# Block 2 moved to the scaled form, and layer 0's weight bound taken from row sums on ScalarE

## The chip, the cores and the metric

The kernel runs on one core of one Trainium2 chip. The metric is the device time of one execution in microseconds (us), from the core's first to its last instruction with the little that lies around it; it is compared as a median of several executions. A core has five engines that work side by side, each through its own instructions in order: TensorE (PE in the profile, matmuls into PSUM), ScalarE (ACT, one function over a tile), VectorE (DVE, elementwise work and reductions), GpSimd (POOL), and SyncE (SP), which here issues most DMAs. An instruction that waits holds back all that stand behind it on its engine.

## The reference, cut to what matters

```
x: (2, 4096, 192)   weight: (8, 7)   w_in: (192, 2048)   w_out: (2048, 192), each layer has its own
w   = softmax(weight)                               # 7 taps per head
x   = causal convolution of x along the 4096 with w, as (8192, 192)
h   = x @ moe_w_in;  g = h * sigmoid(h);  x = g @ moe_w_out                    # layer 0 (SiLU)
h   = x @ moe2_w_in; g = where(h > 0, h, exp(min(h, 0)) - 1); return g @ moe2_w_out   # layer 1 (ELU)
```

All of it is fp32. The kernel keeps fp32 accuracy by splitting each operand of a product in a high part (fp32r, what TensorE reads in one pass) and a low part (the rest), and by adding three products: high by high, high by low and low by high.

## The kernel before

**Tiling.** The 8192 tokens are cut in 16 blocks b of 512, and the 2048 hidden columns in 8 chunks q of 256. A unit (layer, b, q) makes a PSUM tile `h` of 128 x 1024 from the block's tokens and the chunk's `w_in` (18 matmuls of 64 rows by 512 columns, two on the array at a time, L554), then ScalarE and VectorE make `g` in a high and a low part, then TensorE multiplies these by the chunk's `w_out` into sums in PSUM that run over the 8 chunks. `h` has two buffers (`ps_h`, L81): the `in` products of unit s+2 cannot start before unit s's `h` has been read for the last time.

**Two forms of a unit.** The *plain* form (`act_steps`, L579 to L584) makes `hi` and `g` by two SiLU passes on ScalarE and `lo = g - hi` on VectorE, and its `out_products` (L621, L714) are 20 fp32 matmuls. The *scaled* form (L585 to L596) makes one SiLU, then `hi = s * g` (ScalarE, L588), then a 16-bit `lo` (VectorE, L591), with a power of two `s` (`forth`) that keeps `lo` in range. Its `high_products` (L648) are 12 fp32 matmuls; the low products of all 8 chunks are made together at the block's end from 16-bit tiles (`low_products`, L686: 64 matmuls at L671 and L681). `scaled()` (L414) says that all of layer 1 and, in layer 0, the blocks from `NEW` = 3 take this form.

**What the scaled form needs.** For `forth` of a block: a bound on its tokens (`measure`, L432: two VectorE reductions, then a DMA `share` to DRAM and, some steps later, a DMA `fetch` that brings all rows' values to every partition, both on SP's queue) and a bound on the layer's weights. For layer 0's weights `measure_w` (L234) makes 16 reductions on VectorE, `set_weight_scale` (L468) combines them (the tile `own`), and `share` and `fetch` go over GpSimd's queue; `finish_weight_scale` (L479) makes the scales `up` and `down` on VectorE. `set_scale` (L456) makes `forth` and `back`. Each chunk's `w_out` must then be rescaled: `rescale(q)` (L248) has two ScalarE copies (the first makes the 16-bit `w16`), one VectorE instruction (`more`) and two GpSimd additions; `rescale_end(q)` (L261) is one more ScalarE copy. A block's sums are taken out of PSUM by `end_steps` and `emit_end_c`.

**Order.** The order is written out by hand. `units` (L825) lists the units of all blocks, and step s of the program emits the `in` products of unit s. Blocks 0 and 1 go in turn, one chunk each (steps 0 to 15); block 2 has steps 16 to 23 (`TWO` = 16), block 3 steps 24 to 31, and so on. In steps 3 to 18 `both_products` (L1085) interleaves unit s's `in` products with the `out` products of unit s-3. `pair_products` (L714) lets the two row halves of the array add into the same bank, so the second half must come after the first: SP carries a small instruction (`mark`, L743) that waits for a matmul of the first half, and a matmul of the second half waits for that mark. There are three marks a step, in SP's order among its DMAs. From step 20 the loop (L1134) emits `in` products of s, then the work hung into the step by `at(step, f)` (`run_fill`), then the activation of s, then the `out` or `high` products of unit s-2, and of s-3 after the step `turn` = 26 (`LAG` = 2, `LATE` = 3, L822).

Within steps 4 to 18 each step goes: matmuls; in even steps to 12 `decode_steps` of chunk s/2+1, 64-bit data to fp32: ScalarE writes the scratch tile `mag` (L144), VectorE makes two parts (L147, L151) and joins them with `mag` (L155), which is the last to read it; in odd steps `split_w` (two ScalarE copies, three GpSimd subtractions); then what is hung into the step; then the activation. All chunks of layer 0 use one and the same `mag` (`mag_0`, L980). In these steps ScalarE's two SiLUs of unit s free its `h`, since `g` goes to SBUF (`in_tmp`); from step 19 on `g` stays in `h`, and VectorE's `lo` frees it. The plan hangs the 14 taps of block 2's convolution into steps 6 to 13 and those of block 3 into 14 to 20 (`spread`, L871), with the split of the block in high and low (`split_conv`) at the end; block 2's crossing DMAs are put into `pending` and go out behind marks.

Of the kernel before, what the change touches and what calls it, by code (L numbers as in the profile page):

```python
# [9 lines left out]
F32 = mybir.dt.float32  # L10
# [35 lines left out]
def kernel(  # L46
# [184 lines left out]
        t = w16_t[layer, q] = w16_p.tile([P, 2, D], F16, tag=f"w16_{layer}_{q}", name="w16")  # L231
        return t

    def measure_w(q):  # L234
        wi, wo = wt[0, q]
        for k, w in enumerate((wi[:, 0, :], wo[:, :, 0:D])):
            nc.vector.tensor_reduce(
                out=found[:, k, q : q + 1], in_=w.bitcast(F32), axis=AX.X if k == 0 else AX.XY, op=ALU.max,
                apply_absolute_value=True,
            )  # L240
# [592 lines left out]
    def at(step, f, part=0):  # L833
        fill.setdefault((max(step, 0), part), []).append(f)
# [28 lines left out]
    for b in range(2, NB):  # L863
        s = where[0, b, 0]
        if b > 2:
            at(s - 14, lambda b=b: pending.extend(x_loads(b)) if b < 5 else load_x(b))
        steps = [f for fs in zip(*(conv_steps(b, g) for g in range(2))) for f in fs]
        found_it = [lambda b=b: measure(0, b, conv_t[b, 0], conv_t[b, 1])]
        splits = [lambda b=b, g=g: split_conv(b, g) for g in range(2)]
        if b <= 3:  # L870
            spread(steps + found_it * (b == NEW) + splits, s - 10, 7 if b > 2 else 8)  # L871
        elif b == 4:
            for k, f in enumerate(steps):
                at((22, 22, 22, 23, 23, 23, 24, 24, 24, 24, 25, 26, 27, 27)[k], f)
            at(s - 5, found_it[0])
        else:
            for k, f in enumerate(steps):
                step = s - 8 if k < 1 else s - 7 if k < 2 else s - 6
                at(step, f, 0 if k < 5 else 1 if k < 10 else 2)
            at(s - 5, found_it[0])  # L880
        if b >= NEW:
            soon = b in (4, 5)
            at(s - 3 - soon, lambda b=b: fetch((0, b)))
            at(s - 1 - soon, lambda b=b: set_scale(0, b))
        if b >= 4:
            for f in splits:
                at(s - 4, f)
# [3 lines left out]
        at(where[1, b, 0] - 4 - (b == 0), lambda b=b: fetch((1, b)))  # L891
        at(where[1, b, 0] - 2, lambda b=b: set_scale(1, b))
    for q in range(NQ):
        at(TWO - 2 + q // 3, lambda q=q: measure_w(q))
    at(TWO, lambda: set_weight_scale(0, found))
    at(TWO + 1, lambda: fetch(0, nc.gpsimd))
    at(TWO + LAG, lambda: finish_weight_scale(0))
# [25 lines left out]
    with tc.manual_schedule():  # L923
# [301 lines left out]
```

## Time and profile before

| | |
|---|---|
| time, median of 3 (lowest, highest) | 1072.87 us (1072.59, 1072.89) |
| profiled execution: time, span | 1072.07 us, 1070.4 us |
| PE busy | 1065.1 us (100%) |
| DVE busy | 820.0 us (77%) |
| ACT busy | 814.1 us (76%) |
| POOL busy | 89.7 us (8%) |
| granted TensorE clock | 1.000 (mean of the span) |

The profile covers one execution. Times are counted from the span's start. Busy time is when an engine had an instruction at work; matmuls overlap, so that of PE is not a measure of how well it is used: here two matmuls run at a time, and what a group of them takes is read from the start of one group to the start of the next. The difference of 1.7 us between the profiled execution's time and its span lies outside the kernel's instructions.

### The profile page before, as it was taken

What the parts mean: (1) busy time and instruction counts of PE and PEld (TensorE: products, weight loads), DVE (VectorE), ACT (ScalarE), POOL (GpSimd) and SP (SyncE); (2) the same over time, 40 slices, a digit from 0 to 9 for tenths busy, and PEclk for the clock granted to TensorE, in tenths of its full rate; (3) what the DMA queues carried; (4) which work ended last, traced back from release to release, by engine and by line L of the source; (5) the groups of instructions that cost most, each with busy time, mean ns of one, the idle gap of its engine ahead of it and who ended that gap; (6) DMA issues with size and microseconds to landing.
All of it is one profiled execution on the core that took longest, in us unless ns stands there. A gap on an engine that the chain in (4) does not pass through costs nothing.

```text
span 1070.4 us, 23207 instructions
## 1 busy us (share of the span) xinstructions
PE 1065.1 (100%) x9763; PEld 830.7 (78%) x9763; DVE 820.0 (77%) x1123; ACT 814.1 (76%) x908; POOL 89.7 (8%) x139
## 2 busy tenths in 40 slices
PE   9999999999999999999999999999999999999998
PEld 6999977777778777777777787777777777877776
DVE  8998867887877878777467777777777777777766
ACT  7766866666667766677688888888988888888885
POOL 5521121100111011100100000000000000000000
PEclk9999999999999999999999999999999999999999
DMA  6423156424333342323641122311122211222100
GB/s 163 134 46 85 31 137 156 124 71 99 99 109 95 95 116 85 111 76 85 188 123 36 26 59 60 60 41 44 37 60 60 59 37 26 60 60 60 40 13 19
DMA packets 48760, 82.64 MB, mean 77 GB/s; under 512 B 10576, under 2 KB 22736, under 8 KB 48656
## 3 DMA queue, kind: packets, MB, share of 16 engines
q1 hardware_dynamic: 42416, 57.30, 22.1%
q0 software_dynamic: 6240, 23.86, 7.4%
q8 instruction: 76, 1.25, 0.6%
q14 instruction: 28, 0.23, 0.1%
HBM read 43.23 MB, written 18.12 MB: 57 GB/s over the span
## 4 chain that ended last, share of the span: by engine, by line
PE 97%; DMA 1%; DVE 1%; SPq 0%; ACT 0%; issue 0%; DVEq 0%
PE h L554 48%; PE ab L659 20%; PE c L659 10%; PE ab L681 9%; PE c L671 5%; PE ab L734 2%; PE c L734 1%; PE ab L640 1%; PE c L640 1%; DMA raw<-in_w_dram 0%; PE last L698 0%; DMA x_hl<-x_hl 0%; SPq L304 0%; DVE lo L591 0%; ACT x L1013 0%
## 5 line engine op out<-in xcount | busy, mean ns | idle before, releaser
L554 PE MATMUL h<-x_hl,wi 64*128 64x512 f32 x4464 | 575.4, 389 | 0.4 <-DMA x_hl<-x_hl 0.2
L554 PEld LDWEIGHTS h<-x_hl,wi 64*128 64x128 f32 x4464 | 438.4, 184 | 85.5 <-DMA x_hl<-x_hl 0.7
L600 DVE SCALAR_TENSOR_TENSOR g<-g,h 128x1024 f32<-128x1024 f32 x128 | 156.3, 1221 | 127.6 <-ACT g L599 127.6
L659 PE MATMUL ab<-g_hi,wo 64*128 64x512 f32 x1856 | 248.1, 386 | 0.0
L659 PEld LDWEIGHTS ab<-g_hi,wo 64*128 64x128 f32 x1856 | 174.0, 184 | 36.5
L591 DVE SCALAR_TENSOR_TENSOR lo<-h,forth,g_hi 128x1024 f16<-128x1024 f32 x104 | 133.4, 1282 | 84.5 <-ACT g_hi L588 84.0
L596 ACT ACTIVATE h<-h 128x1024 f32<-128x1024 f32 x104 | 104.8, 1008 | 86.0 <-PE h L554 85.9
L591 DVE SCALAR_TENSOR_TENSOR lo<-g,forth,g_hi 128x1024 f16<-128x1024 f32 x128 | 163.6, 1278 | 0.0
L598 ACT ACTIVATE g<-h 128x1024 f32<-128x1024 f32 x128 | 131.6, 1028 | 39.2 <-PE h L554 39.2
L659 PE MATMUL c<-g_hi,wo 64*128 64x512 f32 x928 | 143.2, 386 | 0.0
L588 ACT ACTIVATE g_hi<-g,forth 128x1024 fp32r<-128x1024 f32 x126 | 143.1, 1136 | 0.0
L599 ACT ACTIVATE g<-g 128x1024 f32<-128x1024 f32 x128 | 135.7, 1060 | 4.1
L588 ACT ACTIVATE g_hi<-h,forth 128x1024 fp32r<-128x1024 f32 x104 | 116.2, 1117 | 3.4
L681 PE MATMUL ab<-lo,w 64*128 64x512 f16 x900 | 102.2, 377 | 0.0
L659 PEld LDWEIGHTS c<-g_hi,wo 64*128 64x128 f32 x928 | 87.0, 184 | 18.5 <-DVE g_hi L607 0.2
L509 DVE SCALAR_TENSOR_TENSOR conv<-x_raw,tap_w,conv 128x512 f32<-128x512 f32 (+1 forms) x174 | 100.5, 632 | 0.2
L681 PEld LDWEIGHTS <-w 64*128 64x128 f16 x900 | 41.4, 94 | 58.2 <-issue 11.8
L671 PE MATMUL c<-lo,w 64*64 64x512 f16 x928 | 55.7, 379 | 0.0
L671 PEld LDWEIGHTS <-w 64*64 64x64 f16 x928 | 24.5, 106 | 27.4 <-issue 10.2
L581 ACT ACTIVATE g_hi<-h 128x1024 fp32r<-128x1024 f32 x22 | 22.5, 1023 | 23.7 <-PE h L554 23.7
L789 ACT ACTIVATE mid_ab<-ab,back 128x512 f32<-128x512 f32 x13 | 9.0, 690 | 35.1 <-PE ab L681 35.1
L789 ACT ACTIVATE o<-ab,back 128x512 f32<-128x512 f32 x16 | 11.0, 690 | 32.2 <-PE ab L681 28.4
(132 smaller groups left out, 844.2 us busy)
## 6 DMA issues: line engine op xcount, KB each, us to landing
x_hl<-x_hl SPq DMA_DIRECT2D x60, 256.0 KB, 3.8
raw<-in_w_dram POOLq DMA_DIRECT2D x16, 512.0 KB, 4.6
x_raw<-in_xT_dram SPq DMA_DIRECT2D x16, 259.0 KB, 4.3
kept_ab<-mid_ab SPq DMA_DIRECT2D x16, 256.0 KB, 2.1
raw<-in_w_dram POOLq DMA_DIRECT2D x32, 128.0 KB, 3.7
mid_ab<-kept_ab SPq DMA_DIRECT2D x16, 256.0 KB, 5.1
mid_c<-kept_c SPq DMA_DIRECT2D x32, 128.0 KB, 5.0
x_hl<-x_hl SPq DMA_DIRECT2D x30, 128.0 KB, 3.8
```

Of the source, the lines that this page charges most:

```text
L509: nc.vector.scalar_tensor_tensor(out=y, in0=x, scalar=w, in1=y, op0=ALU.mult, op1=ALU.add)
L554: nc.tensor.matmul(out=h[:, r, :], lhsT=w[ROWS[r], w_lo, ts(of, P)], rhs=x_part(layer, b, 3 * x_lo + part)[ROWS[r], :], start=n == 0, stop ...
L588: nc.scalar.activation(out=hi, in_=g, func=ACTF.Copy, scale=s)
L591: nc.vector.scalar_tensor_tensor(out=lo, in0=g, scalar=s, in1=hi.bitcast(F32), op0=ALU.mult, op1=ALU.subtract)
L596: return [lambda: begun.append(nc.scalar.activation(out=g, in_=h, func=ACTF.Silu)), high, low]
L598: lambda: begun.append(nc.scalar.activation(out=g, in_=h, func=ACTF.Relu, scale=-1.0)),
L599: lambda: nc.scalar.activation(out=g, in_=g, func=ACTF.Exp, scale=-1.0),
L600: lambda: nc.vector.scalar_tensor_tensor(out=g, in0=g, scalar=-1.0, in1=h, op0=ALU.add, op1=ALU.max),
L659: nc.tensor.matmul(out=acc_t[layer, b, f"{name}{r}"], lhsT=wo[ROWS[r], i, ts(k, P)], rhs=hi[ROWS[r], i, :], start=q == 0 and n in (0, 2), ...
L671: nc.tensor.matmul(out=acc_t[layer, b, f"c{r}"][ROWS[i], :], lhsT=w16_t[layer, q][ROWS[r], i, P:D], rhs=g_t[u][1][ROWS[r], i, :], start=Fa ...
L681: nc.tensor.matmul(out=acc_t[layer, b, f"ab{r}"], lhsT=w16_t[layer, q][ROWS[r], i, 0:P], rhs=g_t[u][1][ROWS[r], i, :], start=False, stop=l ...
L734: ins = nc.tensor.matmul(out=acc_t[0, b, name][0 : cols.stop - cols.start, :], lhsT=wo[ROWS[r], i, cols], rhs=g_t[0, b, q][part][ROWS[r], ...
```

## The change

`NEW` becomes 2, so block 2 takes the scaled form: 8 units lose 8 of their 20 `out` matmuls, and `low_products` stands at the block's end. Block 2's tokens are measured (step 12), its `share` and `fetch` (step 13) go over SP, and its scales are set in step 15, behind that step's other work. The weight bound is no longer the maximum over the weights (16 reductions on VectorE in steps 14 to 16) but the largest sum of magnitudes of a row: `sum_w(q)` on ScalarE, one ACTIVATE over 128 x 768 that also gives its sum, or for chunks 0 to 2 (whose decoded tile is gone by then) two over 128 x 384. Their elementwise output goes into `mag`, where nobody reads it. They stand in steps 7, 9, 11, 6, 8, 10, 12, 13 for q = 0 to 7. `set_weight_scale`, `fetch` and `finish_weight_scale` move from steps 16, 17, 18 to 13, 14, 15. `rescale(q)` moves from steps 19 to 24, 28 and 30 to steps 16 to 23, and `rescale_end(q)` to the step after each. The weight `fetch` gets a tile of its own. Around step 19 the `out` products of units 16 and 17 give way to the `high` products of unit 16, so that the lag of three steps begins with block 2; `turn` falls on step 18, where it has no effect.

```
--- before.py
+++ after.py
@@ -36,7 +36,8 @@
 PLACES = NQ + 1
 LINE = 128
 C_LO = HP + 2
-NEW = 3
+NEW = 2
+EARLY = 3
 RING = 11
 EXP = 0x7F800000
 TINY = 2.0**-60
@@ -231,13 +232,21 @@
         t = w16_t[layer, q] = w16_p.tile([P, 2, D], F16, tag=f"w16_{layer}_{q}", name="w16")
         return t
 
-    def measure_w(q):
+    sums = []
+
+    def sum_w(q):
+
+        mag, val = dec_t[0, q]
         wi, wo = wt[0, q]
-        for k, w in enumerate((wi[:, 0, :], wo[:, :, 0:D])):
-            nc.vector.tensor_reduce(
-                out=found[:, k, q : q + 1], in_=w.bitcast(F32), axis=AX.X if k == 0 else AX.XY, op=ALU.max,
-                apply_absolute_value=True,
-            )
+        if q < EARLY:
+            of = [(t[:, IN], w.bitcast(F32)) for t, w in ((mag, wi[:, 0, :]), (mag, wo[:, :, 0:D]))]
+        else:
+            of = [(mag, val.bitcast(F32))]
+        for to, w in of:
+            if len(w.shape) == 3:
+                to = to.rearrange("p (i d) -> p i d", d=D)
+            nc.scalar.activation(out=to, in_=w, func=ACTF.Abs, accum_out=found_0[:, len(sums) : len(sums) + 1])
+            sums.append(q)
 
     def measure_raw(q):
         t = raw_t[1, q].bitcast(F32).rearrange("p (g n two) -> p g n two", g=2, two=2)
@@ -262,6 +271,7 @@
         nc.scalar.activation(out=wt[0, q][1][:, :, 0:D], in_=w16_t[0, q], func=ACTF.Copy)
 
     found = fixed.tile([P, 2, NQ], F32, name="found")
+    found_0 = fixed.tile([P, NQ + EARLY], F32, name="found_0")
 
     tap_raw = const.tile([P, 2, TAPS], F32, name="tap_raw")
     tap_e = const.tile([P, 2, TAPS], F32, name="tap_e")
@@ -425,7 +435,7 @@
         queue.dma_start(out=shared[key].rearrange("a (p n) -> (a p) n", n=2), in_=t)
 
     def fetch(key, queue=nc.sync):
-        t = fixed.tile([P, 2 * P], F32, tag="all", name="all")
+        t = fixed.tile([P, 2 * P], F32, tag="all" if type(key) is tuple else "every", name="all")
         queue.dma_start(out=t, in_=shared[key].to_broadcast([P, 2 * P]))
         shared[key] = t
 
@@ -868,7 +878,7 @@
         found_it = [lambda b=b: measure(0, b, conv_t[b, 0], conv_t[b, 1])]
         splits = [lambda b=b, g=g: split_conv(b, g) for g in range(2)]
         if b <= 3:
-            spread(steps + found_it * (b == NEW) + splits, s - 10, 7 if b > 2 else 8)
+            spread(steps + found_it + splits, s - 10, 7 if b > 2 else 8)
         elif b == 4:
             for k, f in enumerate(steps):
                 at((22, 22, 22, 23, 23, 23, 24, 24, 24, 24, 25, 26, 27, 27)[k], f)
@@ -881,7 +891,7 @@
         if b >= NEW:
             soon = b in (4, 5)
             at(s - 3 - soon, lambda b=b: fetch((0, b)))
-            at(s - 1 - soon, lambda b=b: set_scale(0, b))
+            at(s - 1 - soon, lambda b=b: set_scale(0, b), int(b == NEW))
         if b >= 4:
             for f in splits:
                 at(s - 4, f)
@@ -891,14 +901,13 @@
         at(where[1, b, 0] - 4 - (b == 0), lambda b=b: fetch((1, b)))
         at(where[1, b, 0] - 2, lambda b=b: set_scale(1, b))
     for q in range(NQ):
-        at(TWO - 2 + q // 3, lambda q=q: measure_w(q))
-    at(TWO, lambda: set_weight_scale(0, found))
-    at(TWO + 1, lambda: fetch(0, nc.gpsimd))
-    at(TWO + LAG, lambda: finish_weight_scale(0))
+        at((7, 9, 11, 6, 8, 10, 12, 13)[q], lambda q=q: sum_w(q))
+    at(TWO - 3, lambda: set_weight_scale(0, found_0.unsqueeze(1).to_broadcast([P, 2, NQ + EARLY])))
+    at(TWO - 2, lambda: fetch(0, nc.gpsimd))
+    at(TWO - 1, lambda: finish_weight_scale(0))
     for q in range(NQ):
-        step = TWO + LAG + 1 + q + (q > 5) * (q - 3)
-        at(step, lambda q=q: rescale(q))
-        at(step + 1 + 5 * (q == 5), lambda q=q: rescale_end(q))
+        at(TWO + q, lambda q=q: rescale(q))
+        at(TWO + q + 1, lambda q=q: rescale_end(q))
     looks = [(b, *n) for b in range(3, 6) for n in ((7, 13), (8, 14), (9, 16))][:NQ]
     looks[:3] = (3, 9, 13), (3, 10, 14), (3, 11, 16)
     for q, (b, load, look) in enumerate(looks):
@@ -1124,11 +1133,10 @@
         for f in pending:
             f()
         products(in_products(units[TWO + 3]))
-        products(out_products(units[TWO]))
         act = act_steps(units[TWO + 3])
         run_fill(TWO + 3)
         run(act)
-        products(out_products(units[TWO + 1]))
+        products(high_products(units[TWO]))
 
         turn = where[0, NEW, 0] + LAG
         for s in range(TWO + 4, n_units):
```

## Rows read from the trace of the kernel before

**Rows 1.** The page, busy us (share of the span) and instructions of each engine

```profile
PE 1065.1 (100%) x9763; PEld 830.7 (78%) x9763; DVE 820.0 (77%) x1123; ACT 814.1 (76%) x908; POOL 89.7 (8%) x139
```

**Rows 2.** Windows: stretch, length; busy us of PE, PEld, DVE, ACT, POOL; PEclk; DMA

```profile
77.50:99.60 22.10, 22.10 (x199) 21.86 (x197) 21.51 (x41) 13.21 (x18) 2.30 (x4) 1.00 0.20 61
38.00:90.00 52.00, 52.00 (x462) 51.43 (x460) 48.35 (x69) 31.29 (x40) 16.02 (x15) 1.00 0.25 67
```

**Rows 3.** Timeline of TensorE: start, length, what, count; groups that open steps

```profile
90.53 2.36 PE L554 MATMUL h<-x_hl,wi 64*128 64x512 f32 x18
...
101.41 2.36 PE L554 MATMUL h<-x_hl,wi 64*128 64x512 f32 x18
...
135.81 2.20 PE L554 MATMUL h<-x_hl,wi 64*128 64x512 f32 x18
...
139.21 2.20 PE L554 MATMUL h<-x_hl,wi 64*128 64x512 f32 x18
...
158.03 2.43 PE L554 MATMUL h<-x_hl,wi 64*128 64x512 f32 x18
...
190.69 1.50 PE L554 MATMUL h<-x_hl,wi 64*128 64x512 f32 x10
```

**Rows 4.** Timeline of ScalarE, steps 6 to 8; in brackets the idle time before

```profile
36.98 0.91 ACT L144 ACTIVATE mag<-raw 128x768 f32<-128x768 f32 x1
39.05 1.03 ACT L581 ACTIVATE g_hi<-h 128x1024 fp32r<-128x1024 f32 x1 [1.16 <-PE h L554]
39.97 1.02 ACT L582 ACTIVATE g<-h 128x1024 f32<-128x1024 f32 x1
...
41.31 0.51 ACT L179 ACTIVATE wo<-val 128x384 fp32r<-128x384 f32 x1
43.35 1.03 ACT L581 ACTIVATE g_hi<-h 128x1024 fp32r<-128x1024 f32 x1 [1.53 <-PE h L554]
...
47.66 1.03 ACT L581 ACTIVATE g_hi<-h 128x1024 fp32r<-128x1024 f32 x1 [1.57 <-PE h L554]
```

**Rows 5.** Timeline of VectorE, steps 6 to 8, and block 2's split

```profile
39.89 0.96 DVE L155 SCALAR_TENSOR_TENSOR val<-mag,val 128x768 int32<-128x768 int32 x1
...
45.33 1.23 DVE L583 TENSOR_TENSOR g_lo<-g,g_hi 128x1024 fp32r<-128x1024 f32 x1 [0.66 <-ACT g L582]
46.48 0.61 DVE L147 TENSOR_SCALAR val<-raw 128x768 uint16<-128x768 uint16 x1
...
47.67 0.96 DVE L155 SCALAR_TENSOR_TENSOR val<-mag,val 128x768 int32<-128x768 int32 x1
...
68.21 2.80 DVE L166 TENSOR_TENSOR x_hl<-conv,x_hl 128x512 fp32r<-128x512 f32 x3
```

**Rows 6.** Waits of SP's queue from 20 to 100 us: total, times, longest

```profile
SPq L743 <- PE ab L734: 41.0, 30, 2.2
...
SPq L425 <- DVE sum L435: 3.4, 1, 3.4
```

**Rows 7.** Timeline of VectorE, the weight bound's round trip and unit 19

```profile
85.89 0.17 DVE L471 TENSOR_REDUCE own<-found 128x2 f32<-128x16 f32 x1
...
94.29 0.42 DVE L481 TENSOR_REDUCE most<-all 128x2 f32<-128x256 f32 x1 [0.18 <-DMA all<-shared]
...
98.35 1.22 DVE L583 TENSOR_TENSOR g_lo<-h,g_hi 128x1024 fp32r<-128x1024 f32 x1
```

**Rows 8.** Timeline of ScalarE, the split of block 3 in step 20

```profile
98.19 1.36 ACT L163 ACTIVATE x_hl<-conv 128x512 fp32r<-128x512 f32 x3
```

**Rows 9.** Groups by shape, 0 to 150 us: count, busy us, mean ns, idle before

```profile
L254 DVE SCALAR_TENSOR_TENSOR more<-wo,up,w 128x384 f32<-128x384 f32 x8 | 4.9, 612 | 0.1
L252 ACT ACTIVATE w<-wo,up 128x384 f16<-128x384 f32 x8 | 4.9, 606 | 2.7 <-DVE up L445 2.6
...
L237 DVE TENSOR_REDUCE found<-wi 128x1 f32<-128x384 f32 x8 | 4.3, 544 | 0.0
...
L262 ACT ACTIVATE wo<-w 128x384 fp32r<-128x384 f16 x8 | 4.1, 517 | 0.7 <-DVE more L254 0.6
```

**Rows 10.** One line's instructions: ns min/median/max, start; ScalarE's smallest ACTIVATE

```profile
L279 ACT ACTIVATE tap_e<-tap_e x1: 216/216/216, 3.0 to 3.0; 128x14 f32<-128x14 f32 x1
```

More of the change, by code (lines that the diff above doesn't have):

```diff
@@ L38 @@
 C_LO = HP + 2
-NEW = 3
+NEW = 2
+EARLY = 3
 RING = 11
@@ L232, in new_w16, with sum_w @@
         return t
-    def measure_w(q):
+    sums = []
+    def sum_w(q):
+        mag, val = dec_t[0, q]
         wi, wo = wt[0, q]
[L236 to L240, printed above, removed]
+        if q < EARLY:
+            of = [(t[:, IN], w.bitcast(F32)) for t, w in ((mag, wi[:, 0, :]), (mag, wo[:, :, 0:D]))]
+        else:
+            of = [(mag, val.bitcast(F32))]
+        for to, w in of:
+            if len(w.shape) == 3:
+                to = to.rearrange("p (i d) -> p i d", d=D)
+            nc.scalar.activation(out=to, in_=w, func=ACTF.Abs, accum_out=found_0[:, len(sums) : len(sums) + 1])
+            sums.append(q)
     def measure_raw(q):
@@ L264 @@
     found = fixed.tile([P, 2, NQ], F32, name="found")
+    found_0 = fixed.tile([P, NQ + EARLY], F32, name="found_0")
     tap_raw = const.tile([P, 2, TAPS], F32, name="tap_raw")
@@ L427, in fetch @@
     def fetch(key, queue=nc.sync):
-        t = fixed.tile([P, 2 * P], F32, tag="all", name="all")
+        t = fixed.tile([P, 2 * P], F32, tag="all" if type(key) is tuple else "every", name="all")
         queue.dma_start(out=t, in_=shared[key].to_broadcast([P, 2 * P]))
@@ L870 @@
         if b <= 3:
-            spread(steps + found_it * (b == NEW) + splits, s - 10, 7 if b > 2 else 8)
+            spread(steps + found_it + splits, s - 10, 7 if b > 2 else 8)
         elif b == 4:
@@ L893 @@
     for q in range(NQ):
[L894 to L897, printed above, removed]
+        at((7, 9, 11, 6, 8, 10, 12, 13)[q], lambda q=q: sum_w(q))
+    at(TWO - 3, lambda: set_weight_scale(0, found_0.unsqueeze(1).to_broadcast([P, 2, NQ + EARLY])))
+    at(TWO - 2, lambda: fetch(0, nc.gpsimd))
+    at(TWO - 1, lambda: finish_weight_scale(0))
     for q in range(NQ):
-        step = TWO + LAG + 1 + q + (q > 5) * (q - 3)
-        at(step, lambda q=q: rescale(q))
-        at(step + 1 + 5 * (q == 5), lambda q=q: rescale_end(q))
+        at(TWO + q, lambda q=q: rescale(q))
+        at(TWO + q + 1, lambda q=q: rescale_end(q))
     looks = [(b, *n) for b in range(3, 6) for n in ((7, 13), (8, 14), (9, 16))][:NQ]
@@ L1126 @@
         products(in_products(units[TWO + 3]))
-        products(out_products(units[TWO]))
         act = act_steps(units[TWO + 3])
@@ L1130 @@
         run(act)
-        products(out_products(units[TWO + 1]))
+        products(high_products(units[TWO]))
         turn = where[0, NEW, 0] + LAG
```

2 lines of the change are left out of this document (1 added, 1 removed).

## The prediction

> **What bounds the kernel now.** The page's busy times come first [rows 1]: TensorE is busy all the span, VectorE and ScalarE three quarters of it. Second, TensorE's timeline [rows 3]: groups follow each other at even distances, so any matmul taken away shortens the span, and any wait put in front of TensorE lengthens it. Third, windows around the change [rows 2]: from 38 to 90 us VectorE works 48.35 of 52 us and ScalarE 31.29; from 77.5 to 99.6 VectorE works 21.51 of 22.1. The changed steps thus lie where VectorE has nothing to spare, and the question is who then waits for whom in order. Fourth, the timelines of ScalarE and VectorE in steps 6 to 8 [rows 4, 5]: the slack is ScalarE's idle time ahead of each SiLU, 1.16 to 1.57 us a step.
>
> A step up to 18 takes 4.30 us (the SiLUs of units 6, 7, 8 start at 39.05, 43.35, 47.66 [rows 4]); step s+1 opens 0.2 us before unit s's SiLU. Step 19 opens at 90.53 [rows 3]; counted back by 4.307, step 8 opens at 43.15, 10 at 51.76, 12 at 60.37, 13 at 64.68.
>
> **1. Fewer matmuls: -2.4.** From step 19 to block 4's third unit TensorE takes 158.03 - 90.53 = 67.50 us. A scaled block's period is 190.69 - 158.03 = 32.66 [rows 3]. Two of them, without the 0.23 us that the first group after low products is longer (2.43 against 2.20), are 65.1. This also holds the loss around the present switch at step 26.
>
> **2. The sums on ScalarE: +3.2 by step 12.** Chunks 3 to 6 are summed in even steps 6, 8, 10, 12, behind that step's decode, and write `mag`. VectorE's joining instruction (L155) of the next chunk reads `mag`, so the sum waits for it, and the SiLUs, which free `h`, stand behind the sum on ScalarE. Who waits for these: TensorE, two steps on.
>
> A sum over 768 columns has no row. Below: the same ACTIVATE without a sum, 0.91 [rows 4]. Above: one more small instruction for the sum, at most the smallest ACTIVATE's 0.22 [rows 10]. A saving is excluded, as each is an added instruction. I take 0.1, since neighbours on ScalarE overlap by about 0.1 (SiLU starts 39.05 and 39.97, length 1.03), so a sum holds the engine for 0.9 and a pair of SiLUs ends 1.95 after it starts.
>
> Step 6: VectorE's join ends at 39.89 + 0.96 = 40.85 [rows 5]; sum to 41.8, SiLUs to 43.75. Step 8 wanted `h` at 43.15: 0.6 late.
>
> From there a round of two steps goes: ScalarE's two copies 0.83 (the last ends at 41.82, the SiLUs ended at 40.99 [rows 4]), two sums over 384 of 0.5 each (0.52 by the copy of that size [rows 9]), SiLUs 1.95, together 3.8; VectorE's `lo` 1.15, two decode instructions 1.19, join 0.96 [rows 5], 3.3; sum 0.9, SiLUs 1.95. Sum 9.9, where two steps are 8.61: 1.3 late each round, at steps 10 and 12. Unit 8's SiLUs end at 53.7, unit 10's at 63.6. Together 0.6 + 1.3 + 1.3 = 3.2. Without the waits at `mag` the sums would fit in ScalarE's idle time.
>
> **3. Block 2's measure behind SP's marks: +2.5.** In step 12 `share` waits on SP for two reductions on VectorE; such a wait took 3.4 us for block 3, where no marks are left, and marks make up most of SP's waits [rows 6]. Behind it stand step 13's marks, and TensorE's second row half waits for the first of them. Unit 11's SiLUs end 3.8 after 63.6, at 67.3; chunk 7's join at 70.6; one tap and two reductions (0.54 for 384 columns [rows 9]; an estimate of 1.3 for 768 columns and the tap) make 71.9; issuing the DMA 0.4, 72.4. TensorE wants the mark nine pairs, 2.0 us, into step 13: 64.68 + 3.2 + 2.0 = 69.9. So 2.5 late, which covers the 1.3 that ScalarE would cost at step 14. The `fetch` of step 13 waits for the landing on the same queue; I expect it past in time, bounds 0 and 1. Step 14 is then 5.75 us late.
>
> **4. The weight bound's round trip and VectorE's queue: +3.5.** The combined bound `own` follows unit 12's SiLUs (70.6 + 0.9 + 1.95 = 73.5), `lo` 1.15 and block 2's split, 2.8 to 3.1 [rows 5]: at about 77.8. From `own` to the first use of what comes back took 94.29 - 85.89 = 8.4 [rows 7], so VectorE is held at `finish_weight_scale` in step 15 until 86.2. Queued behind it: unit 15's `lo`, the taps, all to unit 19's `lo`. How much is that? Before, the stretch from step 15 to unit 19's `lo` held 21.5 us of VectorE's work [rows 2]. It loses ten reductions and `own` (4.7), gains three `more` (0.53 each after overlap [rows 9]) and block 2's scale (estimate 1.4, six small instructions), and 0.9 of taps stand ahead of the wait: 18.9, with about 1.7 of waiting for ScalarE in units 17 and 19. Unit 19's `lo` ends at 106.8. A scaled step takes 139.21 - 135.81 = 3.40 [rows 3], so TensorE wants unit 19's `h` at 90.53 + 5.75 + 6.8 = 103.1: 3.5 late after rounding. Before, that `lo` ended at 99.6 and was wanted at 101.41 [rows 3, 7]: step 19 held two `out` groups, which was its cover, and is gone.
>
> **5. Rescaling in steps of 3.40 us: +2.9.** ScalarE's step 20 to 23 is an end copy 0.41, two copies 0.51 each, all less the overlap [rows 9], SiLU and `hi` 1.05 each (an estimate from the 1.02 of a SiLU over the same tile [rows 4]): 3.5 against 3.40, so 0.1 late in steps 23 and 24; step 20 also has block 3's split of 1.36 [rows 8], which makes step 22 1.5 late. In steps 23 and 24 VectorE has block 3's scale and seven taps ahead of `lo`: step 25 is 1.2 late. Then block 2's low products (5.1 us of TensorE alone) let both engines catch up.
>
> **Nothing, with what hides it.** GpSimd's additions are done two steps ahead of their `high` products; GpSimd is nearly idle there [rows 2]. `rescale_end` likewise. PSUM is emptied at block 2's end under the low products, as at block 3's. If that cover failed, it would cost under 1 us.
>
> **Sum.** 3.2 + 2.5 + 3.5 + 2.9 - 2.4 = +9.7. From the profiled execution's 1072.07 that is 1081.8; the median lies 0.8 above that execution, so 1082.5.
>
> **Unknown sizes.** The sum's price of 0 to 0.22 more moves this by -1 to +1.2 (seven sums gate a step). The round trip may be 1 shorter or longer, one to one. Block 2's split is slow in its row, 2.8 us for three instructions [rows 5], beside GpSimd's work; if it and the taps of odd steps go at full speed, 1.2 less.
>
> **Rivals.**
> A. VectorE's relief wins, *not slower*. Sixteen reductions at 0.46 (0.54 less overlap [rows 9]) free VectorE 7.4 us in steps 14 to 16, and ScalarE has 20.7 us idle from 38 to 90 [rows 2]; if VectorE's decode did not stand behind the preceding `lo`, unit 8's SiLUs would end at 48.63 + 0.9 + 1.95 = 51.5, before 51.76, and with the switch covered too only part 1 is left: 1070.4. It decides at `mag`: if the joins come 2.2 us earlier than I have them. Against it: VectorE is strictly in order, and the freed time lies behind steps 6 to 13. The Trainium skill says in "Perfetto Trace Analysis", Optimizing Scalar/DVE Operations, that when VectorE is saturated, moving work to ScalarE may make sense; by that rule alone the time would be this rival's. The busy shares agree with it, the order of waits does not.
> B. Half of it: either the sums fit in, and the switch alone costs (own early, waits of 6.1, less 2.4: +3.7, 1076.5), or the sums cost 5.75 and the switch nothing (+3.4, 1076.2). For it: each part is gated by a chain of its own. Against: both chains are made of measured lengths.
> C. The clock falls. TensorE would idle 2.5 and 3.5 us in one piece; all windows of before show a granted clock of 1.00 [rows 2], with no such idle piece. If it stayed at 1.2 GHz as long as the longer gap, work of 1.75 us would be lost: 1084.3. The Trainium skill, "TensorE: Matmul & The Clock Gate", HAM oscillation, states that idle gaps bring the low level back; no run here shows it.
>
> **Chances.** Forecast (7 to 12 more) 0.68; B 0.20; A 0.07; C 0.05. About 0.2% (2.1 us) is the least a measurement can tell. Faster: A less a little, 0.06. Same: 0.03. Slower: the rest, 0.91. The range leaves out A and the lower half of B, and reaches past C and a dear sum: 1077 to 1085.5.
>
> **What would show it.** Step 8, 10, 12 opening late by 0.6, 1.3, 1.3, with ScalarE's sums waiting for L155 (2); TensorE idle about 2.5 us in the middle of step 13, with SP waiting for the `sum` tile (3); VectorE idle before the weight bound's first use and unit 21's products waiting for unit 19's `lo` (4); shorter waits of the next units (5); then the same periods of 32.66. Wrong if TensorE's steps 6 to 18 keep 4.30 us, or if unit 21 starts on time.

## The result: slower by 1.17%, and where the 12.5 us lie

The changed kernel takes 1085.27 us (median of 4 runs, 1084.86 to 1086.06), the kernel before 1072.82 in the same runs (1072.59 to 1072.89): ratio 1.0117, 95% interval 1.0100 to 1.0135. That is 12.45 us more, where 9.7 were forecast. The rows below come from one profiled execution of each kernel, 1084.86 and 1072.07 us.

The first row of the page after (answers to [rows 1]): busy us, share of the span and instructions of each engine.

```profile
PE 1067.3 (99%) x9763; PEld 815.6 (75%) x9763; DVE 816.7 (75%) x1115; ACT 822.6 (76%) x930; POOL 92.3 (9%) x139
```

VectorE has 3.3 us less to do and ScalarE 8.5 more: their shares of the span move by 2 points at most. TensorE still issues 9763 matmuls: the low products at block 2's end are as many instructions as before, but take less of its time, so "fewer matmuls" in the prediction was the wrong name for a right figure (below).

TensorE's timeline of the kernel after: rows ahead of which it had stood still (start, length, what, count, in brackets the idle time and its releaser), and two that answer to [rows 3].

```profile
72.59 0.50 PE L744 MATMUL c<-g_hi,wo 64*128 64x512 f32 x1 [1.46 <-SPq L753]
...
85.52 0.50 PE L564 MATMUL h<-x_hl,wi 64*128 64x512 f32 x1 [1.25 <-DMA x_hl<-x_hl]
...
101.41 0.73 PE L669 MATMUL c<-g_hi,wo 64*128 64x512 f32 x3 [0.77 <-DVE other L774]
...
109.44 2.35 PE L564 MATMUL h<-x_hl,wi 64*128 64x512 f32 x18 [2.73 <-DVE lo L601]
...
114.32 2.34 PE L564 MATMUL h<-x_hl,wi 64*128 64x512 f32 x18 [1.17 <-DVE lo L601]
...
125.79 2.34 PE L564 MATMUL h<-x_hl,wi 64*128 64x512 f32 x18 [0.81 <-DVE lo L601]
...
170.60 2.43 PE L564 MATMUL h<-x_hl,wi 64*128 64x512 f32 x18
...
203.25 2.43 PE L564 MATMUL h<-x_hl,wi 64*128 64x512 f32 x18
```

The brackets name, in order: a mark on SP (step 13), a DMA that crosses block 2's tokens (unit 17), VectorE's emptying of PSUM (the first `high` group), and three times `lo` on VectorE (units 21, 22 and 25, which wait for that of units 19, 20 and 23). After block 2 all goes as before: at unit 35, the prediction's "block 4's third unit" (counted from one it is the fourth), the distance is 12.57 us (170.60 against 158.03), and 12.56 a block later (203.25 against 190.69).

How late each unit's first in-product starts, after minus before, gives the account by place. From step 20 on the gain has to be added back: 3.17 by step 20 and 0.9 at each step to 26, all but 2.38 of it returned by the low products at block 2's end.

| place | lateness after minus before | cost, us |
|---|---|---|
| steps 8, 10, 12 (0.16 of it from the start) | 0.94, 2.26, 3.58 | 3.42 |
| step 14 | 5.83 | 2.25 |
| unit 17 | 7.43 | 1.60 |
| step 20 | 5.83 | 1.57 |
| unit 21 | 8.03 | 3.10 |
| unit 22 | 8.60 | 1.47 |
| units 23, 24, 25, 26 | 7.83, 6.99, 7.15, 6.38 | 0.13, 0.06, 1.06, 0.13 |
| gain | 12.57 at the end | -2.38 |

This says where TensorE stood, not what each cause is worth alone; the experiments show that the places share causes.

ScalarE's timeline of the kernel after in steps 6 to 8 (answers to [rows 4]).

```profile
41.03 0.85 ACT L248 ACTIVATE mag<-val 128x768 f32<-128x768 f32 x1 [2.98 <-DVE val L156]
41.78 0.19 ACT L248 ACTIVATION_READ_ACCUMULATOR mag<-val 128x1 f32 x1
41.87 1.01 ACT L591 ACTIVATE g_hi<-h 128x1024 fp32r<-128x1024 f32 x1
...
50.96 0.85 ACT L248 ACTIVATE mag<-val 128x768 f32<-128x768 f32 x1 [2.57 <-DVE val L156]
```

The idle time that stood ahead of the SiLU (1.16 to 1.57) now stands ahead of the sum, 2.98 and 2.57 long: ScalarE has time, but waits in order for VectorE's join (L156 here), with the SiLU behind it. The sum holds the engine for 0.84 (41.03 to 41.87), with the extra instruction that reads the sum out.

SP's queue of the kernel after from 66 to 80 us, in steps 13 and 14 (start, length, DMAs issued; a fourth crossing follows).

```profile
72.14 0.34 SPq L435 DMA_DIRECT2D shared<-sum  x1
75.30 0.33 SPq L439 DMA_DIRECT2D all<-shared  x1
76.30 3.89 SPq L332 DMA_DIRECT2D x_hl<-x_hl  x3
```

`share` goes out at 72.14, when the measure on VectorE is done, and TensorE's second half of step 13, which needs the mark behind it, starts at 72.59.

VectorE's timeline of the kernel after, the weight bound's round trip and unit 19's `lo` (answers to [rows 7]).

```profile
77.80 0.18 DVE L481 TENSOR_REDUCE own<-found 128x2 f32<-128x22 f32 x1
...
88.60 0.42 DVE L491 TENSOR_REDUCE most<-all 128x2 f32<-128x256 f32 x1 [5.02 <-DMA all<-shared]
...
108.11 1.28 DVE L601 SCALAR_TENSOR_TENSOR lo<-h,forth,g_hi 128x1024 f16<-128x1024 f32 x1 [0.41 <-ACT g_hi L598]
```

`own` starts at 77.80, as forecast to the tenth; the trip from there to the first use of what comes back then took 10.8 instead of 8.4, and VectorE stood 5.02 us at its end. Where it was longer shows in the DMAs issued from 62 to 92 us: tiles, queue, count, KB each, median us from issue to landing. First the kernel before, then the kernel after.

```profile
x_hl<-x_hl SPq DMA_DIRECT2D x2, 256.0 KB, 3.1
x_hl<-x_hl SPq DMA_DIRECT2D x2, 128.0 KB, 2.4
...
all<-shared POOLq DMA_DIRECT2D x1, 128.0 KB, 4.1
shared<-own POOLq DMA_DIRECT2D x1, 1.0 KB, 3.5
```

```profile
x_hl<-x_hl SPq DMA_DIRECT2D x2, 256.0 KB, 5.9
x_hl<-x_hl SPq DMA_DIRECT2D x2, 128.0 KB, 5.6
all<-shared SPq DMA_DIRECT2D x1, 128.0 KB, 4.5
...
shared<-own POOLq DMA_DIRECT2D x1, 1.0 KB, 6.4
```

The crossings and the 1 KB of the weight bound all take 2.8 to 3.2 us longer to land than before, with one fetch more in the stretch: block 2's 128 copies of 1 KB, issued at 75.30, just ahead of the crossings.

VectorE's first instruction in emptying the PSUM of blocks 0 and 1, in the kernel before, then in the kernel after.

```profile
89.54 0.68 DVE L764 TENSOR_TENSOR other<-c,other 64x512 f32<-64x512 f32 x1
```

```profile
99.36 0.67 DVE L774 TENSOR_TENSOR other<-c,other 64x512 f32<-64x512 f32 x1
```

Before, it began 1.0 us ahead of step 19's in-products (90.53); after, 1.5 us behind them (97.86).

### The profile page after: what moved, and what is told of

Its sections match the earlier page's. It is cut to its first block, busy times and chain, and to the rows that moved or that the text cites. A ratio compares the mean times of both kernels' runs of the same rounds, so it can differ in the third digit from the quotient of the medians.

```text
span 1083.2 us, 23225 instructions
## 1 busy us (share of the span) xinstructions
PE 1067.3 (99%) x9763; PEld 815.6 (75%) x9763; DVE 816.7 (75%) x1115; ACT 822.6 (76%) x930; POOL 92.3 (9%) x139
## 4 chain that ended last, share of the span: by engine, by line
PE 89%; ACT 4%; DVE 3%; DMA 1%; issue 1%; SPq 0%; DVEq 0%; ACTq 0%
PE h L564 44%; PE ab L669 20%; PE c L669 10%; PE ab L691 10%; PE c L681 5%; ACT g_hi L591 1%; ACT g L592 1%; DMA shared<-own 1%; ACT mag L248 1%; ACT g_hi L598 1%; DVE val L156 0%; PE ab L744 0%; ACT h L606 0%; DMA all<-shared 0%; DMA raw<-in_w_dram 0%
## 5 line engine op out<-in xcount | busy, mean ns | idle before, releaser
L669 PE MATMUL ab<-g_hi,wo 64*128 64x512 f32 x1920 | 257.4, 386 | 0.0
L601 DVE SCALAR_TENSOR_TENSOR lo<-h,forth,g_hi 128x1024 f16<-128x1024 f32 x109 | 139.7, 1282 | 92.3 <-ACT g_hi L598 92.0
L669 PEld LDWEIGHTS ab<-g_hi,wo 64*128 64x128 f32 x1920 | 180.1, 184 | 38.2 <-DVE mid_ab L777 0.4
L606 ACT ACTIVATE h<-h 128x1024 f32<-128x1024 f32 x109 | 109.8, 1008 | 89.0 <-PE h L564 89.0
L601 DVE SCALAR_TENSOR_TENSOR lo<-g,forth,g_hi 128x1024 f16<-128x1024 f32 x131 | 167.6, 1280 | 0.2 <-ACT g_hi L598 0.2
L669 PE MATMUL c<-g_hi,wo 64*128 64x512 f32 x960 | 148.9, 387 | 0.8 <-DVE other L774 0.8
L598 ACT ACTIVATE g_hi<-g,forth 128x1024 fp32r<-128x1024 f32 x129 | 146.6, 1136 | 0.1
L598 ACT ACTIVATE g_hi<-h,forth 128x1024 fp32r<-128x1024 f32 x109 | 121.7, 1117 | 3.6
L691 PE MATMUL ab<-lo,w 64*128 64x512 f16 x932 | 105.8, 377 | 0.0
L744 PE MATMUL ab<-g_hi,wo 64*128 64x512 f32 x128 | 35.4, 390 | 0.0
```

Source lines behind the costliest of these rows:

```text
L598: nc.scalar.activation(out=hi, in_=g, func=ACTF.Copy, scale=s)
L601: nc.vector.scalar_tensor_tensor(out=lo, in0=g, scalar=s, in1=hi.bitcast(F32), op0=ALU.mult, op1=ALU.subtract)
L606: return [lambda: begun.append(nc.scalar.activation(out=g, in_=h, func=ACTF.Silu)), high, low]
L669: nc.tensor.matmul(out=acc_t[layer, b, f"{name}{r}"], lhsT=wo[ROWS[r], i, ts(k, P)], rhs=hi[ROWS[r], i, :], start=q == 0 and n in (0, 2), ...
L691: nc.tensor.matmul(out=acc_t[layer, b, f"ab{r}"], lhsT=w16_t[layer, q][ROWS[r], i, 0:P], rhs=g_t[u][1][ROWS[r], i, :], start=False, stop=l ...
L744: ins = nc.tensor.matmul(out=acc_t[0, b, name][0 : cols.stop - cols.start, :], lhsT=wo[ROWS[r], i, cols], rhs=g_t[0, b, q][part][ROWS[r], ...
```

## Experiments

Theory O is the prediction's: four separate waits, each behind an engine that serves in order. In each run "late" means the start of a unit's in-products in that run minus that in the kernel before. Edits are shown shortened; each ratio is to the kernel before, run beside it.

**own_scratch.** The sums write to an unused 16-bit tile instead of `mag`; all else as in the change.

```
-        mag, val = dec_t[0, q]
+        mag, val = junk[0], dec_t[0, q][1]   # junk[0]: ring.tile([P, 2, TB], F16)
```

> The changed kernel, but the sums write their elementwise output into a 16-bit scratch tile of their own (an unused ring slot) instead of `mag`. Theory O (order of waits): the 3.4 us that steps 8 to 12 open late go, since no sum waits for VectorE's join any more; the mark wait in step 13 shrinks to about 1 us, as VectorE's measure comes earlier; later waits stay. About 6 us off the changed kernel's 1085.3: 1079 to 1080. Rival L (load: eleven sums and their accumulator reads are simply too much for ScalarE): steps 8 to 12 stay late, 1085 as before.

1078.88 us, ratio 1.0059 (1.0044 to 1.0074): 0.1 us below O's range and 6 from L's, so O. Steps 8 to 13 are 0.05 late. ScalarE's timeline in step 6:

```profile
37.86 0.84 ACT L251 ACTIVATE junk<-val 128x768 f16<-128x768 f32 x1
38.59 0.20 ACT L251 ACTIVATION_READ_ACCUMULATOR junk<-val 128x1 f32 x1
```

The same instruction, 3.2 us earlier, in what was idle time. Not the sums' 0.84 us cost 3.4, but the buffer that they wrote to. With ScalarE in time, the wait for the mark falls too, from 2.25 to 0.9. This one edit takes the loss from 12.45 to 6.4 us.

**tokens_on_gpsimd.** Block 2's share and fetch go to GpSimd's queue.

```
-        share((layer, b), t)
+        share((layer, b), t, nc.gpsimd if (layer, b) == (0, NEW) else nc.sync)
-            at(s - 3 - soon, lambda b=b: fetch((0, b)))
+            at(s - 3 - soon, lambda b=b: fetch((0, b), nc.gpsimd if b == NEW else nc.sync))
```

> The changed kernel, but block 2's `share` and `fetch` go over GpSimd's queue, so SP's marks stand behind no wait. Theory O: the 1.8 us idle piece in step 13 goes, but ScalarE's round through `mag` then makes step 14 late by 1.3 in its place, and the later queue of VectorE is gated by the same chain: 1084 to 1085.3, a change under 1.5 us. Rival M (the marks cost their 1.8 us and the 1.6 of the late crossings on their own): 1081.9.

1083.87 us, ratio 1.0104 (1.0087 to 1.0121), 0.1 us below O's range and 2 above M's: with ScalarE still late at `mag`, step 14 opens 5.21 late instead of 5.83, and step 15 already 5.73 (0.41 of both is there from the start). Unit 17 no longer waits for crossings; the first `high` group waits more instead, and unit 21 opens 8.03 late, exactly as in the change. (The trace is of the slowest of four executions, 1084.66 us; two took 1083.4, and what differs in them is not shown.) So the places are not additive: unit 21's `lo` comes when VectorE gets to it.

**both_freed.** Both of these.

> The changed kernel with both edits: own scratch for the sums, block 2's `share` and `fetch` on GpSimd's queue. Theory O: steps 6 to 14 open as in the kernel before; what is left is the wait of step 16 for the crossings (0 to 1.6), PSUM's banks at step 19 and units 21, 22 and 25 waiting for VectorE (about 6 in all), less the 2.4 of fewer matmuls: 1077 to 1079.5. Rival: the switch's waits were inherited from the late start, and go too: 1070 to 1072.

1078.65 us, ratio 1.0060 (1.0045 to 1.0075): O. Steps 8 to 16 are 0.12 late; so the whole first part, 5.67 us, and the crossings' 1.6 are gone, and the loss from step 19 on, 6.4 with the gain, stands by itself. It is no clear gain over own_scratch (1078.88), though that still waits 0.9 at the mark and 0.7 at unit 17. The reason is VectorE's order: in the change, own_scratch, tokens_on_gpsimd and both_freed alike it starts to empty PSUM 10.7 to 10.8 us after the first use of the weight bound that came back (88.60, 82.21, 88.61 and 82.43 us) and unit 19's `lo` 19.5 us after it. Whatever TensorE waited for before that, unit 21 opens when this queue has been worked off. TensorE's waits from 30 to 135 us (total, times, longest):

```profile
PE h L567 <- DVE lo L604: 3.5, 2, 2.7
PE c L672 <- DVE other L777: 1.6, 2, 0.9
```

Both name VectorE. In the profiled executions of this run, of tokens_on_gpsimd and of later_rescale TensorE's clock fell after the idle pieces; windows of tokens_on_gpsimd, then of both_freed (stretch, length, busy us of PE, PEld, DVE, ACT, POOL, granted clock, DMA):

```profile
99.60:103.00 3.40, 2.07 (x11) 1.24 (x13) 3.31 (x6) 3.16 (x5) 0.41 (x1) 0.96 0.49 144
103.00:106.50 3.50, 3.50 (x20) 2.75 (x18) 3.50 (x6) 2.03 (x4) 1.89 (x2) 0.55 0.70 200
```

```profile
103.00:106.50 3.50, 3.21 (x20) 2.57 (x22) 2.20 (x5) 3.44 (x6) 1.06 (x2) 0.75 0.32 66
106.50:110.00 3.50, 3.50 (x26) 2.99 (x24) 1.81 (x2) 3.47 (x6) 1.24 (x3) 0.76 0.88 199
```

The stretch from 103.00 to 106.50 in tokens_on_gpsimd holds 20 matmuls, most starting 0.42 us apart in pairs, where 0.23 is usual: the lower level, 1.2 GHz. It is the mechanism of rival C, but the time hardly shows it: unit 21 opens 8.03 late with it (tokens_on_gpsimd) and without it (the profiled execution of the change), as TensorE would only have waited for `lo` in those microseconds; in both_freed unit 22 loses 1.7 where the change loses 1.47.

**sums_alone** and **sums_own_scratch.** The kernel before with the sums and the earlier weight bound only, block 2 unscaled, rescaling at its old steps: first into `mag`, then into a tile of their own.

```
+        at((7, 9, 11, 6, 8, 10, 12, 13)[q], lambda q=q: sum_w(q))
+    at(TWO - 3, ...set_weight_scale)  at(TWO - 2, ...fetch)  at(TWO - 1, ...finish)
```

> The kernel before with one part of the change alone: the sums on ScalarE into `mag` and the earlier weight bound; block 2 stays plain and the rescaling stays at its old steps. Theory O: steps 8, 10, 12, 14 open late by 0.8, 1.3, 1.3, 1.3 and nothing gives it back: 4 to 5 us over the kernel before, 1077 to 1078. Rival A (VectorE's relief wins): 1073 or less.

> The kernel before with ScalarE's sums alone (as sums_alone, 1078.16), written to a scratch tile of their own. Theory O (the sums' 5.1 us in the chunks' steps and the mark wait come only from the shared magnitude buffer, whose last reader VectorE is late): as before, 1072.3 to 1073.2 us. Rival L (the sums' own 7.8 us on ScalarE, or the weight bound's earlier fetch beside the crossings, cost as well): 1074 to 1076.

1078.16 us, ratio 1.0051 (1.0036 to 1.0066), 0.2 above O's range, and 1072.48 us, ratio 1.0001 (0.9992 to 1.0010), O. The first is rival A's test: VectorE has lost its sixteen reductions and nothing is switched, and the kernel is 5.7 us slower. The second shows that the buffer is all of it. It also shows that relief of VectorE by itself is worth nothing measurable here: the move costs 0.2 us (within the interval) with a tile of its own and 5.7 with a shared one. The Trainium skill says in "Perfetto Trace Analysis", Optimizing Scalar/DVE Operations, that when VectorE is saturated, moving some work to ScalarE may make sense; these two runs agree with it only as far as "may".

**later_rescale.** From both_freed: the weight bound's last step on VectorE in step 16, rescaling a step later, block 2's scale behind it.

```
-    at(TWO - 1, lambda: finish_weight_scale(0))
+    at(TWO, lambda: finish_weight_scale(0))
-        at(TWO + q, lambda q=q: rescale(q))
+        at(TWO + q + 1, lambda q=q: rescale(q))
```

> Starts from the kernel with both start costs freed (sums on a scratch of their own, block 2's small transfers on GpSimd; 78.65 over 1000, i.e. 1078.65 us). The weight bound's last step on VectorE is moved from step 15 to step 16, every rescaling one step later, and block 2's scale follows the bound in step 16. Theory O (what is left of the loss is VectorE's queue, held from step 15 until the weight bound's fetch lands and so late with the last low part, with the emptied PSUM banks and with unit 21): the wait at the banks of 1.6 us goes, unit 21's wait shrinks from 3.1 to about 2.4, so 1076 to 1077 us. Rival R (the rescaling's load on ScalarE alone sets the loss, one step sooner or later): 1078 to 1079.5. Rival K (TensorE falls to 1.2 GHz after the idle piece before unit 21 and the stretch at the half clock is the loss): no rows at twice the spacing if the idle piece shrinks, so below 1076.

1076.17 us, ratio 1.0036 (1.0022 to 1.0051): O against R. TensorE's waits from 30 to 135 us:

```profile
PE h L567 <- DVE lo L602: 2.6, 2, 1.8
PE c L671 <- ACT wo L269: 0.7, 1, 0.7
```

VectorE's wait for the PSUM banks is gone; the 0.7 us left there is for a rescaled weight. In both_freed VectorE stood 4.51 us for the weight bound and then came to the banks with one wait of 0.22; here it did not stand, and came there 2.6 us sooner (90.55 against 93.19). So, by the traces, the wait was VectorE's lateness, inherited from the held queue; the edit moved the rescaling too, and no run parts the two. K is out: the idle piece shrank to 1.79 us and the clock fell all the same (18 in-products in 3.21 us), and the two executions with a mean granted clock of 1.000 took as long (1076.17, 1076.22 us) as the three with 0.998 (1076.06 to 1076.30).

**taps_moved.** Block 3's and 4's taps are moved off the steps in which VectorE is late.

```
-        if b <= 3: spread(...)
+        elif b == 3: taps at 14 x5, 15 x5, 16 x2, 17 x2; measure 19; split 20
-  block 4: (22, 22, 22, 23, 23, 23, 24, 24, 24, 24, 25, 26, 27, 27)
+  block 4: (21, 21, 22, 22, 24, 24, 25, 25, 25, 26, 26, 26, 27, 27)
```

> As later_rescale, and block 3's taps on VectorE are brought forward to steps 14 to 17 (its measure to 19, its split to 20), block 4's taps spread over steps 21 to 27 with less of them in steps 22 and 23. Theory O (VectorE is late at unit 21 and ScalarE at unit 22; the first goes with the taps): unit 21's wait falls to about 1.1, unit 25's goes, unit 22's 1.5 stays: 1072.5 to 1074 us. Rival R (ScalarE's rescaling load alone): as later_rescale within 0.5.

1073.10 us, ratio 1.0008 (0.9999 to 1.0018): O. So 3.1 us of what block 2's scaling cost was only where VectorE's other work stood.

**low_on_gpsimd** and **fetch_after.** ScalarE's copy that scales the low part goes to GpSimd; then both fetches are issued behind the last crossing.

```
-        nc.scalar.activation(out=wo[:, :, D : 2 * D], in_=..., func=ACTF.Copy, scale=up[0])
+        nc.gpsimd.tensor_scalar(out=wo[:, :, D : 2 * D], in0=..., scalar1=up[0], op0=ALU.mult)
```

```
+    at(TWO - 1, lambda: (after(nc.gpsimd.nop(), last crossing), fetch(0, nc.gpsimd), fetch((0, NEW), nc.gpsimd)))
```

> As taps_moved, and ScalarE's copy that scales the low part of a weight chunk in each rescaling (0.51 us eight times) is made on GpSimd instead. Theory O (ScalarE's queue was the last thing late at units 21 and 22): its waits shrink to 0.1 and 1.0, and the matmul saved (2.4 us) and what is left give 1070.5 to 1072 us, below the kernel before. Rival G (GpSimd's share of the rescaling, then some 2.7 us of each 3.4 us step, makes the low weights late for the high products): 1073 to 1076.

> As low_on_gpsimd, and GpSimd issues both fetches (the weight bound's and block 2's token sums) only when the last crossing of block 2's tokens has landed. Theory O (the 1.35 us gap in unit 17's step was the crossings, slowed from 2.4-3.1 to 5.4-5.6 us by the fetch of 128 copies issued in the same moment): crossings land in 2.4 to 3.2 us, no gap at unit 17, 1071.0 to 1071.6 us. Rival F (the crossings' slowness has another cause, or the later fetch makes the weight bound and so the rescaling late): gap as before or a new one at the banks or at unit 21, 1072.3 to 1074.

1072.67 us, ratio 1.0002 (0.9992 to 1.0011), between the two ranges; its trace says why: ahead of unit 21 no wait is left (0.99 us in taps_moved) and ahead of unit 22 0.65 (1.17), as O has it, but unit 17 opened 1.3 later, waiting for a crossing. Three of its ten executions took 1071.2 to 1071.4 us, inside O, and seven, the profiled one among them, 1072.6 to 1073.1. fetch_after takes the wait away: 1071.40 us, ratio 0.9992 (0.9983 to 1.0001), as O has it, with all eleven executions from 1071.2 to 1071.6. The DMAs from 62 to 92 us of low_on_gpsimd and of fetch_after:

```profile
x_hl<-x_hl SPq DMA_DIRECT2D x2, 256.0 KB, 5.4
all<-shared POOLq DMA_DIRECT2D x2, 128.0 KB, 4.1
x_hl<-x_hl SPq DMA_DIRECT2D x2, 128.0 KB, 5.6
...
shared<-own POOLq DMA_DIRECT2D x1, 1.0 KB, 6.0
```

```profile
x_hl<-x_hl SPq DMA_DIRECT2D x2, 256.0 KB, 3.5
x_hl<-x_hl SPq DMA_DIRECT2D x2, 128.0 KB, 3.6
all<-shared POOLq DMA_DIRECT2D x2, 128.0 KB, 3.3
...
shared<-own POOLq DMA_DIRECT2D x1, 1.0 KB, 4.6
```

The two differ only in when the fetches are issued, and the crossings land 2 us sooner: it was the fetch that slowed the crossings. When it is issued matters: here it went out with the first crossing (71.13 and 71.14), in taps_moved 0.75 us behind it (71.05 and 70.30), and there the crossings landed after 3.8 and 3.1 us without a wait. Why (a shared DMA engine, the DRAM side) these rows don't tell.

**split_early**, **split_on_gpsimd** and **fetch_before_split.** The split of block 3 is taken off step 20: its ScalarE copies in step 17 (and its taps a step earlier); or these on GpSimd and VectorE's half in step 21 (and block 4's taps later); or that with block 3's fetch ahead of its crossings and three of its taps in step 16 instead of four in 16 and 17.

```
-            for f in splits: at(20, f)
+            at(17, lambda: split_high(3))   # three copies, on ScalarE or on GpSimd
+            at(20, lambda: split_low(3))    # or 21; VectorE's three, and the crossings
```

> As fetch_after, and the ScalarE half of block 3's split (1.36 us in three copies) is made in step 17, where ScalarE waits 1.2 us for TensorE, instead of step 20, its taps a step earlier. Theory O (ScalarE, without a pause from step 18 to 25, is the engine that is late at units 21 and 22, by 0.2 and 0.75): both waits go, 1069.9 to 1070.7 us, under the kernel before by nearly the matmuls saved (2.4). Rival V (VectorE's queue sets those waits): 1071.0 to 1072, as fetch_after.

> As fetch_after, and the three copies of block 3's split are made on GpSimd in step 17 (it has 4 us free there) instead of ScalarE in step 20, VectorE's half of that split goes to step 21 and block 4's taps to steps 22 to 27. Theory O (ScalarE and VectorE, both without a pause from step 18 to 22, are late by 0.2 and 0.75 us at units 21 and 22 because of that split): both waits go, 1070.3 to 1070.9 us. Rival G (GpSimd's copies come between the rescaling's parts and make the low weights late): new waits at the first high products, 1071.5 to 1073.

> As split_on_gpsimd, and block 3's fetch of its token sums is issued a step earlier, ahead of that block's crossings on SP's queue, and its last taps come in steps 15 and 16, so that GpSimd's copies end before the rescaling begins. Theory O (in split_on_gpsimd the wait of 0.75 us at unit 25 is VectorE's, which stood 0.73 us at the fetch that SP issues behind the crossings, and the 0.4 at unit 21 comes from GpSimd's copies beside VectorE's work in step 17): both go, 1070.5 to 1071.2 us, the first below the kernel before by more than its interval. Rival V (VectorE's queue has no room in steps 16 to 22 whatever stands in it): 1071.4 to 1072.2.

split_early: 1072.86 us, ratio 1.0006 (0.9997 to 1.0015), a miss on both sides: TensorE waits for the banks again. The row of its waits that names them:

```profile
PE c L690 <- DVE other L795: 0.8, 1, 0.8
```

VectorE now stands 1.41 us for ScalarE ahead of unit 17's `lo` (in fetch_after it does not) and comes to the banks at 92.42 instead of 89.88: ScalarE's idle time in step 17 was slack for what VectorE does next, not free time. split_on_gpsimd: 1072.17 us, ratio 0.9998 (0.9989 to 1.0007), a miss for O and inside G's range, but not by G's mechanism, as the first `high` group waits for nothing: unit 22's wait goes, as O has it, 0.24 us is left at unit 21, and unit 25 now waits 0.70, since block 3's scale does (VectorE's timeline):

```profile
109.11 0.42 DVE L490 TENSOR_REDUCE total<-all 128x1 f32<-128x256 f32 x1 [0.73 <-DMA all<-shared]
```

SP issues that fetch behind the crossings, which now come a step later. fetch_before_split issues it ahead of them: **1070.65 us, ratio 0.9984 (0.9975 to 0.9993)**, the one version whose whole interval lies below the kernel before, by 1.67 us of the 2.4 that there were; at 0.16% it is a small gain. Its page and TensorE's timeline at units 21 and 22:

```profile
PE 1063.1 (99%) x9763; PEld 819.3 (77%) x9763; DVE 817.4 (76%) x1115; ACT 817.8 (77%) x919; POOL 106.6 (10%) x152
```

```profile
97.76 2.33 PE L586 MATMUL h<-x_hl,wi 64*128 64x512 f32 x18
101.29 1.98 PE L586 MATMUL h<-x_hl,wi 64*128 64x512 f32 x16
```

No bracket is left at either, where the change has 2.73 and 1.17.

## Why the prediction was right, and by how much its terms were off

- **1, the gain: right.** -2.4 forecast; of step 20's 3.17 and 0.9 a step, 2.38 stay. It was taken from the periods of blocks in [rows 3], not from a count of matmuls, and the count indeed stayed at 9763.
- **2, the sums: right.** 0.6, 1.3, 1.3 forecast, 0.78, 1.32, 1.32 measured, and own_scratch shows that `mag` is the cause. The sum's unknown price came out at 0.84 for 768 columns, below the 0.9 taken; its ACTIVATE alone, 0.85 long, is shorter than the 0.91 that was to be the least.
- **3, the mark: right in place, and in size with its neighbour.** 2.5 forecast, 2.25 measured; together with 2 the step 14 opened 5.83 late against 5.75. The `share` goes out at 72.14, ends at 72.48 (72.4 forecast). The idle piece is 1.46, not 2.5. Alone the mark is worth little: where it is taken away (tokens_on_gpsimd), step 15 opens 5.73 late instead of 5.83, because ScalarE at `mag` is late by nearly as much. The prediction says that the mark "covers" that wait; the reverse holds as well.
- **3, the fetch: mis-sized.** "I expect it past in time, bounds 0 and 1" was asked of SP's queue only. TensorE stood for it, 1.6, but not because it held SP: it slowed the crossings issued next, from 2.4 to 3.1 us up to 5.6 to 5.9. That wait adds nothing to the end, since unit 21 opens just as late without it.
- **4, VectorE's held queue: right in mechanism, its trip mis-sized.** 3.5 forecast at unit 21 (its own figures, 106.8 less 103.1, give 3.7), 3.1 measured, though by two errors that met: the trip took 2.4 longer, where a bound of 1 was given, and TensorE came 3.2 later by the terms missed at unit 17 and at the banks. The 1 KB of `own` landed after 6.4 instead of 3.5 us, beside the crossings and block 2's fetch; no run shows which of these slowed it.
- **5, rescaling: right.** 2.9 forecast, 2.85 measured (1.47, 0.13, 0.06, 1.06, 0.13), unit 22 and 25 carrying it.
- **"Nothing", PSUM: failed.** "PSUM is emptied at block 2's end under the low products" looked at the wrong end. What has to be emptied in time is the pair's PSUM of blocks 0 and 1, since block 2's first group opens the same banks behind unit 19's in-products; VectorE, held by the weight bound in step 15, now reaches that late (99.36 against in-products that start at 97.86). TensorE lost 1.57 there, over the "under 1 us" allowed, and the wait went in later_rescale when VectorE's queue was let go.

By place, the two missed terms, 1.6 and 1.57, less the 0.4 or so by which the others were high, are most of the 2.75 us between 9.7 and 12.45. By cause it is one term: unit 21 opens when VectorE's queue has been worked off, and that queue was let go 2.4 us later than forecast (88.60 against 86.2); what followed in it took 20.8 us to the end of unit 19's `lo`, where 20.6 were forecast. The prediction had said that the trip counts "one to one".

That the measured time lies inside the stated range, 0.2 us below its upper end, is in part luck: that end was set for a clock that falls and a dear sum, and what filled the room was the longer trip; one of the four executions, 1086.06, lies above it.

Rival A fell with sums_alone. B fell too: both halves of the loss came. With the sums freed the switch still costs 6.4 us (own_scratch, 3.7 in B). The sums without the switch cost 5.7 (sums_alone), the 5.75 of B; its +3.4 has a gain of 2.4 taken off, which that kernel does not have.

Rival C's clock stays at 1.00 in all windows of the change's profiled execution, with an idle piece of 2.73 us, and falls in those of three experiments, after pieces of 0.86, 0.76 and 2.72 (both_freed), of 0.65 and 1.79 (later_rescale) and of 1.06 and 0.76 (tokens_on_gpsimd). But the other three executions of the change have a mean granted clock of 0.998, as these three have, so it most likely fell there; no trace of them is kept. They took 0.3 to 1.2 us longer than the one at 1.000, less than C's 1.75 and with a single execution to compare. The Trainium skill states in "TensorE: Matmul & The Clock Gate", HAM oscillation, that idle gaps bring the low level back; the traces agree in three executions and not in the fourth.

## What to carry to other kernels

An added instruction on an engine with idle time is priced by what it waits for and by who stands behind it: the output that nobody reads needs a tile of its own. When a step is brought forward, list each transfer that it brings forward with it, and look what lands in the same microseconds. Waits that one queue sets do not add up: look for the place where they meet, here unit 21, and ask what arrives there last. And where a cover is claimed ("under the low products"), name the first instruction that needs the result, since it may stand at the other end of the block.

## What the runs showed of the hardware

- A fetch of one 1 KB row to 128 partitions (3.2 to 4.6 us itself) slows SBUF to SBUF crossings when it is issued with or ahead of the first of them: they landed after 4.7 to 6.0 us (the change, own_scratch, low_on_gpsimd). Issued 0.75 to 1.2 us behind the first, it left them at 2.9 to 4.8 (tokens_on_gpsimd, both_freed, later_rescale, taps_moved); without it they took 2.4 to 3.6 (the kernel before, fetch_after, split_on_gpsimd).
- A 1 KB store to DRAM landed after 3.5 us with no crossing beside it (the kernel before), after 4.5 and 4.6 beside crossings alone (split_on_gpsimd, fetch_after), and after 4.6 to 6.4 beside crossings and the fetch.
- A sum along the columns on ScalarE is a second instruction, ACTIVATION_READ_ACCUMULATOR, 0.18 to 0.20 long; ahead of a SiLU it held the engine for 0.09 (41.78 to 41.87), ahead of another sum for 0.23 (44.92 to 45.15, the kernel after).
- TensorE fell to 1.2 GHz after idle pieces of 0.65 and 1.79, of 1.06 and 0.76, and of 0.86, 0.76 and 2.72 us, in three profiled executions, and not in the change's after 0.77 and 2.73. In later_rescale the time was the same with and without the fall.
